# Two small TensorE steps of a Fourier-filter and MLP kernel put into one gap

## The chip, the cores and the metric

The kernel runs on one core of a Trainium2 chip. The metric is the device time of one execution in microseconds, the median of several runs. The core has a matrix engine (TensorE, PE in the profile, with its weight loads as PEld), VectorE (DVE), ScalarE (ACT), GpSimd (POOL) and SyncE (SP), which here only issues DMAs. TensorE writes into eight PSUM banks; VectorE and ScalarE read them out.

## The reference

Eight batches of 3008 tokens with 256 channels each are filtered along the tokens in the frequency domain, and every token then goes through a two-layer MLP with the activation h - tanh(h):

```python
X = np.fft.rfft(x, axis=1)                         # x: (8, 3008, 256)
y = np.fft.irfft(X * (filt_r + 1j * filt_i), n=3008, axis=1)
h = y.reshape(24064, 256) @ w_in                   # (256, 2048)
out = (h - np.tanh(h)) @ w_out                     # (2048, 256)
```

## The kernel before

The transform of length 3008 = 64 x 47 is done as matrix products in three stages. The **first stage** transforms along 64 (`first(b, z)`, six steps for a batch, its products into tiles called `pf`) and stores its result in DRAM (`ct1`). The **middle stage** (`middle(b, z)`) loads it, transforms along 47, multiplies with the filter and transforms back; it has four rounds of ten steps for a batch: "there" (products into four banks), eight filter steps on VectorE, "back" (products into four banks), and its result goes to DRAM again (`ct2`). The **last stage** (`last(i, z)`) loads one group's part of that (`e2`, and a table `gt`), transforms back along 64 (products into `pu`) and so makes the MLP's input `ut` for one group of tokens, with four sums of its blocks (`tu`) on GpSimd.

The MLP is the bulk. Its tokens are cut into 48 groups, six of each batch (c = 0 to 5), of 512 tokens (448 in the first group, c = 0, whose products are 224 wide and not 256). A group is worked off in four units (u = 0 to 3) of a quarter of the hidden width each. Both layers are done by a seven-product scheme for 2 x 2 blocks, so that sums of blocks are needed beside the products: `tu` before the first layer and `t` before the second, both on GpSimd by `combine` (L543 to L546, four subtractions one after another).

Three units are in work at a time. In turn U, `up(U)` makes the first layer's products into the banks x, y and z (L563), `shrink(U - 1)` does the activation (three ScalarE functions L675, L678, L681; a VectorE multiplication L685 for each half; and at its end, behind the second half, the four `t` sums on GpSimd), and `down(U - 2)` makes the second layer's products into the banks o0 to o3 (L733). In the last unit of a group these banks are read out as soon as they are complete, in the turn that is unit 1 of the next group; the last of these sums is L767 on GpSimd, and `store` then transposes the two halves of the output on VectorE (L813) in unit 2 and queues its DMAs.

The order of all engines is written out by hand: each engine works off its instructions in the order in which the program issues them. `up` calls `t(k)` at five places of a unit; these places are the **gaps** (u, k) into which the Fourier steps are put. For a unit of batches 1 to 7 the order is: X1, Y2, `t(0)`, second-layer products, `t(1)`, X6, Z5, second-layer products, `t(2)`, X7, second-layer products, X4, `t(3)`, the last part of the activation, second-layer product 4, `t(4)`, Z3. (X, Y, Z name the bank; Z3 adds onto the bank that L603 reads in between, Z + u3.) At every gap the stores queued by the first stage (`written`) are issued by ScalarE and four of the other queued stores (`outs`) by SyncE.

In batches 1 to 5 a group holds these steps:

- first stage of the batch after next: gap (0, 2), into the banks t and y
- middle stage of the next batch: "there" in (2, 0) of groups 0 to 3, into t, o3, o1, o2; filter steps in gaps of units 2, 3, 0 and 1; "back" in (1, 3) of groups 1 to 4, into o0, t, y, o1. So group 0 has no "back", and group 5 has no step of the middle stage at all
- last stage of the next group: gap (3, 2), into t and y

The first stage's steps do two 64-row halves at once, eight matmuls of 64x64 by 256 columns (L296); one bank is copied by ScalarE (L301), and VectorE takes sum and difference (L302, L303). The last stage's step is 32 matmuls of 64x64 by 64 columns (L522), read out in the same way (L526, L529, L530).

Loads: `load_e2` for the next group is issued at the head of unit 0, but at the head of unit 2 where the next group begins a batch. In unit 2 of group 5 the first loads of the next `middle` and the next `first` are issued too; each further step of `first` issues the loads of the step after next.

Of the kernel before, what the change touches and what calls it, by code (L numbers as in the profile page):

```python
# [9 lines left out]
F32 = mybir.dt.float32  # L10
# [7 lines left out]
BATCH, SEQ, DM = 8, 3008, 256  # L18
# [8 lines left out]
NC = NH // CH  # L27
# [84 lines left out]
def kernel(  # L112
# [32 lines left out]
    groups = [(b, c) for b in range(BATCH) for c in range(NC)]  # L145
# [363 lines left out]
    e2s, uts = {}, {}  # L509
# [425 lines left out]
    with tc.tile_pool(name="tr", bufs=2) as tr, tc.manual_schedule():  # L935
# [257 lines left out]
        with tc.tile_pool(name="dn", bufs=2) as dn, \  # L1193
                tc.tile_pool(name="ps", bufs=1, space=bass.MemoryType.PSUM) as ps:

            def zd(name, shape):
                return ps.tile(shape, F32, tag="t", bufs=1, name=name)

            def zd2(name, shape):
                return [ps.tile(shape, F32, tag=tag, bufs=1, name=name) for tag in "ty"]  # L1200

            def zd4(tags):
                return [ps.tile([128, 2, DM], F32, tag=tag, bufs=1, name="pm") for tag in tags]

            psums.append(zd)
            pairs_of.append(zd2)

            y_sums = dn.tile([128, 2 * 4 * len(groups)], F32, bufs=1, name="y_sums")

            def psl(shape, tag):  # L1210
                return ps.tile(shape, F32, tag=tag, bufs=1, name="pt")

            def filters_d():
                zero = tr.tile([128, 2, DM], F32, tag="e1", bufs=2, name="zero")
                G.memset(zero, 0.0)
                row = 4 * DM
                nc.sync.dma_start(dram(filt_d, 2 * DM, [[PAD * row, 31], [1, 2 * DM]]),
                                  zero[0:31].rearrange("p a n -> p (a n)"))
                for k in range(4):
                    nc.sync.dma_start(dram(filt_d, (NH + 2 * k) * row,  # L1220
                                           [[PAD * row, 32], [2 * DM, 4], [1, 2 * DM]]),
                                      zero.rearrange("p a n -> p (a n)"))
                yield
                for at in range(8):
                    a = 8 * (at // 2) + at % 2
                    n = 4 if at < 7 else 3
                    for v, src in enumerate((filt_r.tensor, filt_i.tensor)):
                        base = at * 128 * row
                        nc.sync.dma_start(dram(filt_d, base + v * DM,
                                               [[row, NH], [PAD * row, n], [1, DM]]),  # L1230
                                          dram(src, (a + 1) * DM,
                                               [[NQ * DM, NH], [2 * DM, n], [1, DM]]))
                        yield
                        nc.sync.dma_start(dram(filt_d, base + row + (2 + v) * DM,
                                               [[row, NH - 1], [PAD * row, n], [1, DM]]),
                                          dram(src, (NQ - a - 1) * DM,
                                               [[NQ * DM, NH - 1], [-2 * DM, n], [1, DM]]))
                        yield
                        if n == 3:
                            nc.sync.dma_start(dram(filt_d, turned * row + v * DM,  # L1240
                                                   [[row, NH], [1, DM]]),
                                              dram(src, 0, [[NQ * DM, NH], [1, DM]]))

            bound = bounded()
            copies = filters_d()
            total = 4 * len(groups)
            for _ in last(0, z2):
                pass
            warm = psl([128, 256], "o3")
            for _ in range(4):  # L1250
                nc.tensor.matmul(warm[0:KM], mats[:, 3 * KM:4 * KM], mats[:, 3 * KM:3 * KM + 256],
                                 start=True, stop=True)
            G.dma_start(mats[:, 0:10 * PAD], wide_d[0:KM])
            for _ in range(4):
                next(late)
            due = [4 + (LEAD - 4) * k / (NX + 4) for k in range(NX + 4)]
            plan = []
            kinds = {(2, 0): "there", (1, 3): "back"}
            kinds.update({at: "filter" for at in FILTERED})

            firsts, mids = {2: fs}, {}
            for U in range(total + 2):
                i, u = divmod(U, 4)
                if U == 6:
                    assert not pending
                    late = sums(7)
                if U < total:
                    p, c = groups[i]
                    if c == 0 and u == 0 and 0 < p < BATCH - 1:
                        plan += STAGES  # L1270
                    if u == 0 and i + 1 < len(groups) and c + 1 < NC:
                        e2s[i + 1] = load_e2(*groups[i + 1])
                    if u == 2 and i + 1 < len(groups) and c + 1 == NC:
                        assert not plan
                        e2s[i + 1] = load_e2(*groups[i + 1])
                    if u == 2 and c + 1 == NC:
                        for gens, ahead, what in ((mids, 2, middle), (firsts, 3, first)):
                            if p + ahead < BATCH:
                                gens[p + ahead] = what(p + ahead, zd4 if what is middle else z2)
                                next(gens[p + ahead])  # L1280
                sh = shrink(U - 1) if 0 <= U - 1 < total else iter(())
                dw = iter(())
                if 0 <= U - 2 < total:
                    dw = (down if U - 2 >= 4 else down_plain)(U - 2)

                def converting(n):

                    for _ in range(n):
                        if next(late, pending) is pending:
                            pending.clear()  # L1290

                def d():

                    next(dw, None)

                def e():

                    next(dw, None)
                    converting(3 if U > 1 else 1)

                def s():

                    next(sh, None)

                def t(k):

                    while written:
                        ACT.dma_start(*written.pop(0))
                    store_some(4)
                    if k == 2 and stores:  # L1310
                        store(*stores.pop())
                    if U >= total:
                        return
                    pos = 20 * c + 5 * u + k
                    if i == 1 and pos == LEAD - 7:
                        mids[1] = middle(1, zd4)
                        next(mids[1])
                        plan.extend(STAGES)
                    if (u, k) == (3, 2) and i + 1 < len(groups):
                        next(last(i + 1, z2))  # L1320
                    elif due and due[0] <= pos and (U < 4 or u < 3 and k == 2):
                        due.pop(0)
                        next(firsts[2])
                    elif (u, k) == (0, 2) and 0 < p < BATCH - 2:
                        next(firsts[p + 2])
                    elif plan and plan[0] == kinds.get((u, k)):
                        plan.pop(0)
                        next(mids[p + 1])
                    converting(2)
                    if k and U > 1:  # L1330
                        next(copies, None)

                if U < total:
                    if U == total - 1:
                        ones = cst.tile([128, 1], F32, name="ones")
                        G.memset(ones, 1.0)
                    (up if U >= 4 else up_plain)(U, d, e, s, t)
                else:
                    for k in range(5):
                        s()  # L1340
                        s()
                        d()
                        if U == total + 1 and k in (0, 2):
                            next(bound)
                        e()
                        t(k)
            for w in stores:
                store(*w)
            store_some(len(outs))
# [36 lines left out]
```

## Time and profile before

| what | value |
|---|---|
| time, median of 3 runs | 2607.54 us (2607.4 to 2609.2) |
| profiled execution, its own time | 2605.47 us |
| span of the profiled execution | 2603.7 us |
| mean granted TensorE clock | 0.995 |
| busy: TensorE / VectorE / ScalarE / GpSimd | 2568.3 / 1911.0 / 1668.0 / 1378.7 us |

A line of a timeline gives the start in us from the begin of the span, the duration in us, the engine, the source line, the operation with the tiles that it writes and reads, and in brackets how long the engine was idle before and what ended that. In the chain (the work that ended last, in order of time) a line is start, duration, engine, tile, source line and the number of records. A line of waits is: engine, its tile and line, `<-`, what it waited for; then us in total, times, and the longest. A float32 matmul leaves two records, so "x4" of L563 is one product of two matmuls. A matmul's record ends after its successor has begun; the chain counts from start to start.

### The profile page before, as it was taken

The numbers are of one execution on the slowest core, as the hardware profiler recorded it, in microseconds if no ns is written. First come the engines' busy times: TensorE is split into PE (matmuls) and PEld (weight loads), VectorE is DVE, ScalarE is ACT, GpSimd is POOL, SyncE is SP. The second block draws the span as 40 slices with busy tenths as digits, with TensorE's granted clock in tenths as the row PEclk, the third lists the DMA queues.
The fourth block names the chain that finished last, engine by engine and source line by source line (L and its number), as shares of the span: only waits on it lengthen the run. The fifth ranks groups of instructions, "written<-read, shape, count | busy, mean of one in ns | idle before, by whom it ended". The sixth has DMA issues, their size and how long they took to land.

```text
span 2603.7 us, 47351 instructions
## 1 busy us (share of the span) xinstructions
PE 2568.3 (99%) x18276; PEld 2201.7 (85%) x18276; DVE 1911.0 (73%) x2514; ACT 1668.0 (64%) x2594; POOL 1378.7 (53%) x1087
## 2 busy tenths in 40 slices
PE   8998999999999999999999999999999999999998
PEld 7677888888898888988889888888889888898887
DVE  6787886888668885788758887588866888555555
ACT  4565666666666666666666666666666666666665
POOL 4114664565546554555555555455654665555552
PEclk9999999999999999999999999999999999999999
DMA  8853315332323323333233432333221331110110
GB/s 224 258 165 99 87 25 124 94 104 61 92 64 106 95 60 82 91 86 98 49 88 84 110 76 55 94 95 93 74 71 41 78 81 36 39 34 18 24 22 18
DMA packets 347852, 214.49 MB, mean 82 GB/s; under 512 B 242179, under 2 KB 315791, under 8 KB 347553
## 3 DMA queue, kind: packets, MB, share of 16 engines
q1 hardware_dynamic: 331601, 174.98, 27.0%
q10 hardware_dynamic: 11632, 23.11, 2.8%
q0 software_dynamic: 4384, 13.29, 1.7%
q8 instruction: 146, 2.39, 0.4%
q14 instruction: 89, 0.73, 0.1%
HBM read 130.72 MB, written 83.39 MB: 82 GB/s over the span
## 4 chain that ended last, share of the span: by engine, by line
PE 94%; DMA 2%; DVE 2%; ACT 1%; POOL 1%; issue 0%; SPq 0%; ACTq 0%; DVEq 0%; POOLq 0%
PE o L733 42%; PE x L563 25%; PE z L563 12%; PE y L563 6%; PE pm L340 3%; PE pu L522 2%; PE pf L296 1%; PE o L788 1%; DMA filt<-in_filt_r_dram 1%; DMA ct<-a 0%; DMA x<-in_x_dram 0%; PE pf L284 0%; DMA ct<-nn 0%; PE o L633 0%; DMA ct<-e 0%
## 5 line engine op out<-in xcount | busy, mean ns | idle before, releaser
L733 PE MATMUL o<-t,wd 128*128 128x256 f32 (+1 forms) x3008 | 762.4, 376 | 0.1
L543 POOL TENSOR_TENSOR t<-h 128x512 f32<-128x512 f32 (+1 forms) x186 | 292.7, 1574 | 761.3 <-DVE h L685 757.4
L685 DVE TENSOR_TENSOR h<-h,y 128x1024 f32<-128x1024 f32 (+1 forms) x384 | 530.8, 1382 | 141.4 <-ACT y L681 140.9
L733 PEld LDWEIGHTS o<-t,wd 128*128 128x128 f32 x3008 | 569.1, 190 | 75.2 <-issue 9.9
L563 PE MATMUL x<-tu,wu 128*128 128x256 f32 (+1 forms) x2256 | 579.0, 379 | 0.0
L733 PE MATMUL o<-h,wd 128*128 128x256 f32 (+1 forms) x2256 | 572.8, 376 | 1.8 <-DVE h L685 1.8
L569 ACT COPY s<-x 128x512 f32<-128x512 f32 (+1 forms) x188 | 108.6, 578 | 602.1 <-PE x L563 571.6
L733 PEld LDWEIGHTS o<-h,wd 128*128 128x128 f32 x2256 | 426.0, 190 | 62.4 <-issue 11.5
L563 PEld LDWEIGHTS x<-tu,wu 128*128 128x128 f32 x2256 | 421.0, 190 | 65.1 <-issue 12.0
L678 ACT ACTIVATE y<-y 128x1024 f32<-128x1024 f32 (+1 forms) x384 | 399.3, 1040 | 12.1
L675 ACT ACTIVATE y<-h 128x1024 f32<-128x1024 f32 (+1 forms) x384 | 400.9, 1044 | 3.6 <-DVE h L611 1.7
L681 ACT ACTIVATE y<-y 128x1024 f32<-128x1024 f32 (+1 forms) x384 | 399.7, 1041 | 5.0 <-ACT a L286 0.4
L544 POOL TENSOR_TENSOR t<-h,t 128x512 f32<-128x512 f32 (+1 forms) x186 | 275.3, 1480 | 14.6
L545 POOL TENSOR_TENSOR t<-h 128x512 f32<-128x512 f32 (+1 forms) x186 | 279.9, 1505 | 0.0
L546 POOL TENSOR_TENSOR t<-h,t 128x512 f32<-128x512 f32 (+1 forms) x186 | 260.6, 1401 | 0.0
L569 ACT COPY u<-x 128x512 f32<-128x512 f32 (+1 forms) x376 | 213.4, 568 | 56.4 <-PE x L563 53.6
L611 DVE COPY h<-x 128x512 f32<-128x512 f32 (+1 forms) x188 | 127.8, 680 | 123.4 <-PE x L563 122.3
L563 PE MATMUL z<-ut,wu 128*128 128x256 f32 (+1 forms) x752 | 191.1, 377 | 9.1 <-DVE h L603 9.1
L563 PE MATMUL x<-ut,wu 128*128 128x256 f32 (+1 forms) x752 | 190.8, 376 | 0.0
L563 PE MATMUL y<-ut,wu 128*128 128x256 f32 (+1 forms) x752 | 190.1, 375 | 0.0
L563 PE MATMUL z<-tu,wu 128*128 128x256 f32 (+1 forms) x752 | 190.0, 375 | 0.0
L586 DVE TENSOR_TENSOR h<-y,s 128x512 f32<-128x512 f32 (+1 forms) x188 | 126.6, 673 | 65.2 <-PE y L563 57.6
(175 smaller groups left out, 2933.4 us busy)
## 6 DMA issues: line engine op xcount, KB each, us to landing
ft<-filt SPq DMA_DIRECT2D x56, 512.0 KB
ct<-nn SPq DMA_DIRECT2D x112, 256.0 KB
e<-ct SPq DMA_DIRECT2D x47, 512.0 KB
a<-ct SPq DMA_DIRECT2D x224, 96.0 KB
out_dram<-ot SPq DMA_DIRECT2D x1248, 16.0 KB
x_sb<-in_x_dram SPq DMA_DIRECT2D x74, 256.0 KB
ct<-a ACTq DMA_DIRECT2D x62, 256.0 KB
gt<-g_pairs SPq DMA_DIRECT2D x42, 128.0 KB
```

The source lines that it names most:

```text
L543: by.tensor_sub(t[0], b[0][1], b[0][0])
L544: by.tensor_sub(t[1], b[1][1], t[0])
L545: by.tensor_sub(t[2], b[1][1], b[0][1])
L546: by.tensor_sub(t[3], b[1][0], t[1])
L563: nc.tensor.matmul(bank[:, k], wu[:, q - 1, (2 * u + k) * 128:(2 * u + k + 1) * 128], rhs[q - 1], start=(first and k == 0), stop=True, ski ...
L569: ACT.copy(t, X)
L611: V.tensor_copy(h[:, 2, :, 0:w], X)
L675: ACT.activation(y[k], ht[k], AF.Arctan, scale=TURN)
L678: ACT.activation(y[k], y[k], AF.Tanh, scale=BEND)
L681: ACT.activation(y[k], y[k], AF.Square, scale=SCALE, accum_out=y_sums[:, 2 * U + k // 2:2 * U + k // 2 + 1])
L685: V.tensor_mul(ht[k], ht[k], y[k])
L733: nc.tensor.matmul(product(q), wd[:, q - 1, (2 * u + k) * 128: (2 * u + k + 1) * 128], rhs[q - 1][:, k], start=(u == 0 and k == 0 and q == ...
```

## The change

In groups 0 and 5 of batches 1 to 5 (ten groups), both the first-stage step, which was in gap (0, 2), and the last-stage step, which was in gap (3, 2), are issued in gap (1, 3), one behind the other. The first-stage step keeps the banks t and y, the last-stage step takes o0 and o1. In groups 1 to 4, and in batches 0, 6 and 7, the two steps stay where they were. With it `load_e2` is issued at the head of unit 0 for the first group of a batch too (but for batch 1's, which stays at unit 2), since the step that reads it comes earlier.

```diff
+            pair = ["ty"]
+
             def zd2(name, shape):
-                return [ps.tile(shape, F32, tag=tag, bufs=1, name=name) for tag in "ty"]
+                return [ps.tile(shape, F32, tag=tag, bufs=1, name=name) for tag in pair[0]]
...
-                    if u == 0 and i + 1 < len(groups) and c + 1 < NC:
-                        e2s[i + 1] = load_e2(*groups[i + 1])
-                    if u == 2 and i + 1 < len(groups) and c + 1 == NC:
-                        assert not plan
+                    if u == (p == 0 and c + 1 == NC) * 2 and i + 1 < len(groups):
+                        assert not plan or c + 1 < NC
                         e2s[i + 1] = load_e2(*groups[i + 1])
...
-                    if (u, k) == (3, 2) and i + 1 < len(groups):
+                    joined = 0 < p < BATCH - 2 and c % (NC - 1) == 0
+                    if joined and (u, k) == (1, 3):
+                        next(firsts[p + 2])
+                        pair[0] = "o0", "o1"
+                        next(last(i + 1, z2))
+                        pair[0] = "ty"
+                    elif (u, k) == (3, 2) and i + 1 < len(groups) and not joined:
                         next(last(i + 1, z2))
                     elif due and due[0] <= pos and (U < 4 or u < 3 and k == 2):
                         due.pop(0)
                         next(firsts[2])
-                    elif (u, k) == (0, 2) and 0 < p < BATCH - 2:
+                    elif (u, k) == (0, 2) and 0 < p < BATCH - 2 and not joined:
                         next(firsts[p + 2])
```

## The prediction

> **What bounds the kernel now.** I read the page's busy shares first, then its chain, then who TensorE waits for (in the stretch from 420 us to 2590 us, where the five changed batches lie), and at last the timeline of the two places that change.
>
> ```profile
> PE 2568.3 (99%) x18276; PEld 2201.7 (85%) x18276; DVE 1911.0 (73%) x2514; ACT 1668.0 (64%) x2594; POOL 1378.7 (53%) x1087
> PE 94%; DMA 2%; DVE 2%; ACT 1%; POOL 1%; issue 0%; SPq 0%; ACTq 0%; DVEq 0%; POOLq 0%
> PE o L733 <- DVE h L685: 1.8, 2, 1.6
> ```
>
> TensorE is busy all the time and the chain is TensorE. The third line is that whole list of TensorE's waits: 1.8 us in two waits. So the change can win only what it takes out of TensorE's own stream, and it loses whatever makes TensorE wait where it does not wait now.
>
> **What a gap costs TensorE.** The chain in order of time, around one last-stage step (`pu`, L522) and one first-stage step (`pf`, L296), each standing alone:
>
> ```profile
> 727.48 1.09 PE pu L522 x64
> 728.57 1.06 PE x L563 x4
> ...
> 731.36 0.86 PE x L563 x4
> ...
> 740.43 1.02 PE pf L296 x16
> 741.46 0.95 PE x L563 x4
> 742.41 1.73 PE o L733 x8
> 744.14 0.76 PE x L563 x4
> ```
>
> The product behind each step is longer than the same product elsewhere: 1.06 for 0.86, 0.95 for 0.76. So `pu` costs 1.09 + 0.20 = 1.29 and `pf` 1.02 + 0.19 = 1.21, together 2.50 us. The change touches ten such pairs.
>
> Back to back, the step into normal products after `pf` goes away: 1.02 + 1.09 + 0.20 = 2.31, 0.19 saved. Perhaps some of the way in goes too. Nothing in this trace has the two steps side by side. Each step by itself reads 1.02 and 1.09; in each quarter of the array both push as many columns as a 256-wide product pair, which takes 0.86, so the joined step lies between 1.72 + 0.20 = 1.92 and the full 2.50. I take 2.24, nearer to the rows as they stand: 0.26 saved for each of ten, 2.6 us in all.
>
> The Trainium skill (TensorEngine Tiling (Array Packing), section Key Properties) says that a change of tiling mode drains the array, and a change of tile alone does not. Both steps are on 64x64 tiles, so by it the junction is free; that is the rival "only the drain", below.
>
> **What follows behind the gap.** The new place is behind the product X4 of unit 1, ahead of the last product of the finished group. First the pace of the evictions, from the two steps as they are now, and the `tu` sums that GpSimd makes of the last stage's result:
>
> ```profile
> 740.36 1.09 PE L296 MATMUL pf<-x_sb,f 64*64 64x256 f32 x16
> 741.52 0.58 ACT L301 COPY other<-pf 128x512 f32<-128x512 f32 x1 [0.56 <-PE pf L296]
> 742.14 0.69 DVE L302 TENSOR_TENSOR a<-pf,other 128x512 f32<-128x512 f32 x1 [1.61 <-ACT other L301]
> 742.75 0.68 DVE L303 TENSOR_TENSOR a<-pf,other 128x512 f32<-128x512 f32 x1
> ...
> 727.41 1.16 PE L522 MATMUL pu<-gt,e 64*64 64x64 f32 x64
> 729.26 0.69 DVE L529 TENSOR_TENSOR ut<-pu,odd 128x512 f32<-128x512 f32 x1 [2.24 <-ACT odd L526]
> 729.87 0.55 DVE L530 TENSOR_TENSOR ut<-pu,odd 128x384 f32<-128x384 f32 x1
> 730.49 0.67 POOL L543 TENSOR_TENSOR tu<-ut 128x224 f32<-128x224 f32 x1 [4.56 <-DVE ut L530]
> 732.47 0.66 POOL L546 TENSOR_TENSOR tu<-ut,tu 128x224 f32<-128x224 f32 x1
> ```
>
> VectorE starts on `pf` 1.78 us after its first matmul and takes 0.61 a step. The second step's copy is ready 1.85 after `pu` starts, which is about 1.0 + 1.85 = 2.85 after `pf` starts, before VectorE has done L302 and L303 (1.78 + 1.22 = 3.0). So four evictions run without a break and L685, the multiplication of unit 1, starts 1.78 + 2.42 = 4.20 after the gap. In both cases `tu` comes about then, and on GpSimd the four `tu` sums now stand **ahead of** the four `t` sums of L685's result, and these ahead of the output sum L767. In the old place, unit 3, the `t` sums were followed by no L767.
>
> Now the first group of a batch (batch 1), as it is:
>
> ```profile
> 443.06 0.92 PE L563 MATMUL x<-tu,wu 128*128 128x224 f32 x4
> 444.59 1.08 DVE L685 TENSOR_TENSOR h<-h,y 128x896 f32<-128x896 f32 x1
> 445.82 1.14 POOL L543 TENSOR_TENSOR t<-h 128x448 f32<-128x448 f32 x1 [1.32 <-DVE h L685]
> 450.32 0.73 POOL L767 TENSOR_TENSOR o<-p,p 128x256 f32<-128x256 f32 x1
> 452.67 1.09 DVE L685 TENSOR_TENSOR h<-h,y 128x896 f32<-128x896 f32 x1
> 453.68 1.30 DVE L813 STREAM_TRANSPOSE ot<-o 128x512 f32<-128x512 f32 x2
> 454.90 1.18 DVE L432 TENSOR_TENSOR nn<-xy,ft 128x1024 f32<-128x1024 f32 x1
> 456.00 0.61 DVE L603 TENSOR_TENSOR h<-z,u 128x448 f32<-128x448 f32 x1
> 457.00 0.92 PE L563 MATMUL z<-ut,wu 128*128 128x224 f32 x4
> ```
>
> The last line, product Z3 of unit 2, writes the bank that L603 reads: it cannot start before L603's end, and the slack today is 457.00 - 456.61 = 0.39 us. L603 stands on VectorE behind the filter step L432, that behind the two transposes L813, and the second transpose needs L767. Today L767 ends at 451.05, and the second transpose comes up at 453.68 + 0.65 = 454.33, 3.3 us later.
>
> How VectorE and GpSimd meet:
>
> ```profile
> 712.59 1.27 POOL L546 TENSOR_TENSOR t<-h,t 128x512 f32<-128x512 f32 x1
> 713.23 1.71 DVE L685 TENSOR_TENSOR h<-h,y 128x1024 f32<-128x1024 f32 x1 [2.19 <-ACT y L681]
> 713.82 1.72 POOL L767 TENSOR_TENSOR o<-p,p 128x256 f32<-128x256 f32 x1
> ...
> 719.49 1.22 DVE L685 TENSOR_TENSOR h<-h,y 128x1024 f32<-128x1024 f32 x1
> ```
>
> L685 takes 1.22 alone and 1.71 here: it ends 1.08 after L546's end (713.86). L767, 0.73 elsewhere, ends at 715.54, so it ran from 714.81: it stood about 0.95 behind L685. One waits for the other in full. The Trainium skill (SBUF — State Buffer, section Who interferes with whom) says the same: a VectorE instruction with two SBUF inputs and a GpSimd one that reads SBUF lock each other out, the earlier one first. Without such holds the two sums below would end 1.8 and 1.9 us earlier, no wait would be left in them, and the change would win 0.26 at each place.
>
> The sum for the first group: `pf` starts behind X4, 443.06 + 0.76 + about 0.1 = 443.9. L685 at 448.1. It holds GpSimd until 449.05 (0.95). Four `tu`: 730.49 to 733.13 is 2.64 for 224 columns; the next group has 256, so 3.0: 452.05. Four `t`: 445.82 to 450.32, 4.5: 456.55. The L685 of unit 2 falls among them and holds them once more, 0.85 for its 896 columns: 457.4. L767 0.73: 458.1. Second transpose 0.65: 458.8. L432 1.10: 459.9. L603 0.61: 460.5. Z3 then starts at 460.5 for 457.00, so 3.5 later; the two steps that are gone from units 0 and 3 give back 2.50. **Net 1.0 us lost.** TensorE by itself would be there at 457.0 + 2.24 = 459.2; it waits 1.3, part of it perhaps earlier, at the middle-stage step at the head of unit 2 (L340), whose bank o3 is read by an add queued behind L685.
>
> The last group (batch 1), which has no filter step in unit 2:
>
> ```profile
> 705.74 1.03 PE L563 MATMUL x<-tu,wu 128*128 128x256 f32 x4
> 708.77 1.27 POOL L543 TENSOR_TENSOR t<-h 128x512 f32<-128x512 f32 x1 [1.60 <-DVE h L685]
> 714.87 1.41 DVE L813 STREAM_TRANSPOSE ot<-o 128x512 f32<-128x512 f32 x2
> 716.91 0.69 DVE L603 TENSOR_TENSOR h<-z,u 128x512 f32<-128x512 f32 x1 [0.64 <-ACT u L569]
> 719.55 1.03 PE L563 MATMUL z<-ut,wu 128*128 128x256 f32 x4
> ```
>
> `pf` at 705.74 + 0.96 = 706.7; L685 at 710.75 (the fourth eviction is the narrow one); GpSimd free at 711.7; `tu` 2.64: 714.35; four `t` 5.05 (708.77 to 713.82): 719.4; one hold 0.95: 720.35; L767 0.73: 721.1; second transpose 0.70: 721.8; L603 0.69: 722.5. Z3 moves by 2.95, less 2.50: **0.45 us lost.** Part of this wait may be met earlier, at the products that read the `t` sums.
>
> Five of each: 5 x 1.45 = 7.3 us. The other batches' rows lie one batch (312 us) on and I take them to be alike.
>
> **Costs taken at nothing.** ScalarE's two evictions: behind them it has nothing to do before the first copy of unit 2, two products later; without that cover their 1.2 us would delay that copy. Its two stores of `a1` wait for L303, and only that copy is queued behind them. The load of the last-stage input `e2` now leaves at the head of unit 0 in both groups. SyncE:
>
> ```profile
> 696.95 3.23 SPq L323 DMA_DIRECT2D a<-ct  x8
> 705.95 0.63 SPq L255 DMA_DIRECT2D x_sb<-in_x_dram  x1
> 715.59 14.51 SPq L840 DMA_DIRECT2D out_dram<-ot  x28
> ```
>
> The loads L323 read what the first stage stores, whose last part now leaves after 706.7 + 3.0 = 709.7, and before in unit 0. So SyncE stands still from 697 to about 712, its 9.6 us of loads end near 722 and the 28 stores run to 737. The loads are read from the middle of the next group on, the stores by nobody. Queued behind them is the `e2` of the next first group, read about 20 us later; that cover gone, the gap there would wait for it, a microsecond for each that it comes late.
>
> **Rivals.** *Only the drain*: GpSimd's lateness is covered, and the kernel is 2.6 us faster: 2604.9. For it: TensorE never waits now, and GpSimd is busy 53%. Against it is the chain above. In the first group it decides if L767 ends by 451.05 + 3.3 + 0.4 + 2.24 = 457.0 (its slack, that of Z3, and TensorE's own shift) and not at 458.1. Chance 0.12. *Half*: the holds overlap or the sums run faster, the first groups lose 0.6 and the last ones win 0.26: 5 x 0.34 = 1.7, 2609.2. Chance 0.2. *More*: VectorE's lateness runs on into the filter steps of unit 3, and the first group loses 2 us instead of 1: 5 x 2.45 = 12.3, 2619.8. For it: these steps fill VectorE there; against: unit 3 is rid of `pu`'s evictions. Chance 0.08. The forecast has 0.6.
>
> **The numbers.** The profiled execution took 2605.5 (span 2603.7); 7.3 on it is 2612.8. The median of the runs is 2607.5, 2.1 above, so the forecast is 2614.8. The range leaves out most of *only the drain* and of *more*: 2607 to 2619. About 0.2%, 5.2 us, is what a measurement can tell from no change: *only the drain* (2.6) and *half* lie within it, with a small part of the forecast; faster by more would need over 0.52 saved a pair, more than a pair has: 0.03. Same 0.35, slower 0.62.
>
> **What would show it.** TensorE waits for L603 before a `z` product ten times, 0.5 to 1.3 us each; `tu` rows on GpSimd straight before `t` rows, the first of them beside L685; L767 some 3 us later against its unit; `pf` and `pu` in one stretch of about 2.1 us. Wrong if TensorE still waits 1.8 us in all, or if the waits are for a DMA.

## The result, and the profile after

The changed kernel takes 2615.6 us (median of 11 runs, 2611.9 to 2618.2) against 2607.6 (11 runs, 2604.8 to 2610.4): 1.0029 times the time of before, 95% interval 1.0022 to 1.0037. The change makes the kernel 8 us slower. The profiled execution has a span of 2612.5 us.

The busy shares and the chain of the page, and TensorE's waits from 420 to 2590 us:

```profile
PE 2570.4 (98%) x18276; PEld 2203.1 (84%) x18276; DVE 1911.4 (73%) x2514; ACT 1668.8 (64%) x2594; POOL 1386.8 (53%) x1087
PE 89%; POOL 4%; DVE 3%; DMA 2%; issue 1%; ACT 1%; SPq 0%; ACTq 0%; DVEq 0%; POOLq 0%
PE z L563 <- DVE h L603: 4.1, 5, 0.8
PE o L733 <- POOL t L545: 1.9, 6, 0.3
PE o L733 <- DVE h L685: 0.2, 1, 0.2
```

TensorE has as much to do as before. GpSimd, which had 1% of the chain, now has 4% of it, VectorE 3% where it had 2%. The waits have the two names that the sum led to: L603, and a `t` sum. Among the waits of TensorE's weight loads, two are new; before, neither is in the list:

```profile
PEld z L563 <- DVE h L603: 7.6, 10, 1.2
PEld pm L340 <- DVE o L766: 1.1, 5, 0.2
```

The first group of batch 1, the timeline around the joined gap:

```profile
442.26 0.92 PE L563 MATMUL x<-tu,wu 128*128 128x224 f32 x4
443.11 1.09 PE L296 MATMUL pf<-x_sb,f 64*64 64x256 f32 x16
444.02 1.11 PE L522 MATMUL pu<-gt,e 64*64 64x64 f32 x64
446.03 0.92 PE L563 MATMUL z<-ut,wu 128*128 128x224 f32 x4
447.29 1.08 DVE L685 TENSOR_TENSOR h<-h,y 128x896 f32<-128x896 f32 x1
447.45 1.51 POOL L543 TENSOR_TENSOR tu<-ut 128x256 f32<-128x256 f32 x1 [3.76 <-DVE ut L530]
448.39 1.79 PE L340 MATMUL pm<-a,mats_sb 24*32 24x256 f32 x64
451.10 1.14 POOL L543 TENSOR_TENSOR t<-h 128x448 f32<-128x448 f32 x1
454.32 1.20 DVE L685 TENSOR_TENSOR h<-h,y 128x896 f32<-128x896 f32 x1
454.52 2.00 POOL L546 TENSOR_TENSOR t<-h,t 128x448 f32<-128x448 f32 x1
456.47 0.73 POOL L767 TENSOR_TENSOR o<-p,p 128x256 f32<-128x256 f32 x1
457.24 0.71 DVE L813 STREAM_TRANSPOSE ot<-o 128x512 f32<-128x512 f32 x1 [1.10 <-POOL o L767]
457.87 1.18 DVE L432 TENSOR_TENSOR nn<-xy,ft 128x1024 f32<-128x1024 f32 x1
458.98 0.61 DVE L603 TENSOR_TENSOR h<-z,u 128x448 f32<-128x448 f32 x1
459.64 1.02 PE L563 MATMUL z<-ut,wu 128*128 128x224 f32 x4 [0.83 <-DVE h L603]
```

To be read from top to bottom as one chain: L685 and the first `tu` sum meet (1.51 for a sum that takes 0.72), the four `tu` sums take until 451.10, the `t` sums follow, the last of them stands behind the next L685 (2.00 for 1.14), L767 comes at 456.47, the second transpose waits 1.10 for it, and Z3 waits for L603. The L340 step at 448.39 takes 1.79. Before, it took 1.49:

```profile
447.04 1.49 PE L340 MATMUL pm<-a,mats_sb 24*32 24x256 f32 x64
```

It has begun, but its products for bank o3 wait: the sum L766, which reads that bank, ends at 448.71, and within the step no weights are loaded from 448.44 to 448.76. In the list of the products this wait does not appear, so that list (6.2 us) is shorter than what is lost.

The last group of batch 1:

```profile
705.97 1.03 PE L563 MATMUL x<-tu,wu 128*128 128x256 f32 x4
718.11 1.26 POOL L545 TENSOR_TENSOR t<-h 128x512 f32<-128x512 f32 x1
719.42 1.56 PE L733 MATMUL o<-t,wd 128*128 128x256 f32 x6 [0.34 <-POOL t L545]
721.31 0.71 DVE L813 STREAM_TRANSPOSE ot<-o 128x512 f32<-128x512 f32 x1 [3.68 <-POOL o L767]
721.95 0.65 DVE L603 TENSOR_TENSOR h<-z,u 128x512 f32<-128x512 f32 x1
722.65 1.13 PE L563 MATMUL z<-ut,wu 128*128 128x256 f32 x4
```

Here the same lateness is met twice: first at the product that reads the third `t` sum, then at Z3, which begins where L603 ends. The eight matmuls from 718.48 on, in which the first wait lies, take 2.34 us where they took 1.72 before; Z3 and the product behind it come another 0.22 late.

For the size, one stretch that holds one last and one first group: from the last "back" step (L340) of a batch to the first one of the next batch. Before, then after, from the timeline of TensorE:

```profile
654.21 1.50 PE L340 MATMUL pm<-xy,mats_sb 24*32 24x256 f32 x64
804.26 1.50 PE L340 MATMUL pm<-xy,mats_sb 24*32 24x256 f32 x64
```
```profile
655.67 1.49 PE L340 MATMUL pm<-xy,mats_sb 24*32 24x256 f32 x64
807.22 1.49 PE L340 MATMUL pm<-xy,mats_sb 24*32 24x256 f32 x64
```

The stretch is 150.05 us before and 151.55 after: 1.50 is lost per batch, 7.5 in five. The stretches of the later batches in each trace agree with this one to 0.03 us, while whole executions of one kernel differ by some 6. So this stretch is the measure for the experiments.

### The profile page after: what moved, and what is told of

Read it like the earlier page. It is cut to its first block, busy times and chain, and to the rows that moved or that the text cites. A ratio compares the mean times of both kernels' runs of the same rounds, so it can differ in the third digit from the quotient of the medians.

```text
span 2612.5 us, 47353 instructions
## 1 busy us (share of the span) xinstructions
PE 2570.4 (98%) x18276; PEld 2203.1 (84%) x18276; DVE 1911.4 (73%) x2514; ACT 1668.8 (64%) x2594; POOL 1386.8 (53%) x1087
## 4 chain that ended last, share of the span: by engine, by line
PE 89%; POOL 4%; DVE 3%; DMA 2%; issue 1%; ACT 1%; SPq 0%; ACTq 0%; DVEq 0%; POOLq 0%
PE o L733 40%; PE x L563 23%; PE z L563 11%; PE y L563 6%; PE pm L340 3%; PE pu L522 2%; PE pf L296 1%; PE o L788 1%; POOL t L544 1%; POOL tu L543 1%; POOL t L543 1%; PE pf L284 1%; POOL t L545 0%; DMA x<-in_x_dram 0%; POOL t L546 0%
## 5 line engine op out<-in xcount | busy, mean ns | idle before, releaser
L685 DVE TENSOR_TENSOR h<-h,y 128x1024 f32<-128x1024 f32 (+1 forms) x384 | 532.0, 1385 | 141.9 <-ACT y L681 141.7
L544 POOL TENSOR_TENSOR t<-h,t 128x512 f32<-128x512 f32 (+1 forms) x186 | 280.3, 1507 | 14.6
L546 POOL TENSOR_TENSOR t<-h,t 128x512 f32<-128x512 f32 (+1 forms) x186 | 270.0, 1451 | 0.0
L603 DVE TENSOR_TENSOR h<-z,u 128x512 f32<-128x512 f32 (+1 forms) x188 | 126.8, 674 | 66.8 <-ACT u L569 64.4
```

Of the source, the lines that this page charges most:

```text
L544: by.tensor_sub(t[1], b[1][1], t[0])
L546: by.tensor_sub(t[3], b[1][0], t[1])
L685: V.tensor_mul(ht[k], ht[k], y[k])
```

## The experiments

**The `tu` sums put back.** The theory is the queue on GpSimd; the rival is that four evictions in one gap make VectorE late by themselves. The gap stays as changed, but the four `tu` sums are issued where they were, in (3, 2) (all line numbers behind are two higher):

```diff
+        uts[i] = (b, tu, w)
+        if late_sums:
+            yield
         combine(b, [tu[:, k, 0:w] for k in range(4)], V if pending else G)
-        uts[i] = (b, tu, w)
         yield
...
-                        next(last(i + 1, z2))
+                        summing = last(i + 1, z2, late_sums=True)
+                        halves[0] = summing
+                        next(summing)
                         pair[0] = "ty"
+                    elif (u, k) == (3, 2) and joined:
+                        next(halves[0])
```

> Both steps in gap (1, 3) as in the change, but the four tu sums are issued in gap (3, 2), where they stood before. Theory (the tu sums queue ahead of the t sums on GpSimd, and so L767, the transposes, L603 and Z3 come late): the waits for L603 and for the t sums go; left are the saving at the junction, about 0.35 us at each place, and in the first group the wait of the middle-stage step for bank o3, about 0.25 us. The stretch from one batch's last back step to the next batch's first one, 150.05 us before and 151.55 changed, becomes about 149.6; the time about 2605.5 (2 us below the kernel before). Rival (four evictions in one gap make VectorE itself late): most of the loss stays, the stretch is above 150.8, the time above 2611.

```profile
654.92 1.49 PE L340 MATMUL pm<-xy,mats_sb 24*32 24x256 f32 x64
804.67 1.50 PE L340 MATMUL pm<-xy,mats_sb 24*32 24x256 f32 x64
448.64 1.79 PE L340 MATMUL pm<-a,mats_sb 24*32 24x256 f32 x64
PE o L735 <- DVE h L687: 1.8, 2, 1.6
```

The stretch is 149.75, the time 2605.3 us (ratio to the kernel before 0.9992, interval 0.9983 to 1.0001: by the time alone it can't be told from the kernel before). The products' waits for L603 and the `t` sums are gone; only the old 1.8 us is listed. In the stretch, the whole loss of 1.50 has turned into a gain of 0.30, with the same four evictions. What is left is the middle-stage step with 1.79: bank o3, as expected. The stretch is still 0.15 longer than expected; the cause of that stays open. The rival falls. The banks o0 and o1 and the earlier `load_e2` are in this run as in the change, so they don't make the loss either.

**One gap later.** Both steps in (1, 4), behind product 4; by then L685, the `t` sums and L767 have been issued. The stores of the first stage are issued at once, since the loads that read them are issued at the head of unit 2:

```diff
-                    if joined and (u, k) == (1, 3):
+                    if joined and (u, k) == (1, 4):
...
+                        while written:
+                            ACT.dma_start(*written.pop(0))
```

> Both steps back to back one gap later, in (1, 4), behind second-layer product 4, with the same four banks; the stores of the first stage's result are issued right behind them. Theory: L685, the t sums, L766 and L767 are now issued ahead of the evictions and of the tu sums, so nothing of the chain is late and o3 is free in time; 0.35 us saved at each of ten places, stretch about 149.35, time about 2604.1. Rival (four evictions in one gap make VectorE late): VectorE has the same four in one gap, Z-bank add and next copies are late, the stretch stays above 150.5.

```profile
655.08 1.49 PE L340 MATMUL pm<-xy,mats_sb 24*32 24x256 f32 x64
804.42 1.49 PE L340 MATMUL pm<-xy,mats_sb 24*32 24x256 f32 x64
445.83 1.14 POOL L543 TENSOR_TENSOR t<-h 128x448 f32<-128x448 f32 x1 [1.33 <-DVE h L685]
449.21 1.49 PE L340 MATMUL pm<-a,mats_sb 24*32 24x256 f32 x64
450.35 0.72 POOL L767 TENSOR_TENSOR o<-p,p 128x256 f32<-128x256 f32 x1
451.04 0.72 POOL L543 TENSOR_TENSOR tu<-ut 128x256 f32<-128x256 f32 x1
```

The stretch is 149.34, 0.71 below that of before, and the time 2603.5 us (ratio 0.9985, interval 0.9976 to 0.9994): faster than both kernels. On GpSimd the order is now `t`, L767, `tu`, and the L340 step is back at 1.49. So the junction by itself saves 0.35 us at each place, and the changed kernel waits 151.55 - 149.34 = 2.21 us in each stretch.

**Each step alone in the gap.** First only the last-stage step in (1, 3), with the first-stage step left in (0, 2); then the other way round:

```diff
-                        next(firsts[p + 2])
...
-                    elif (u, k) == (0, 2) and 0 < p < BATCH - 2 and not joined:
+                    elif (u, k) == (0, 2) and 0 < p < BATCH - 2:
```

> In the ten groups only the last-stage step moves to (1, 3) (banks o0 and o1), the first-stage step stays in (0, 2). No junction, so nothing saved; VectorE has two evictions in the gap and not four. Theory: the tu sums still stand ahead of the t sums, and both ends of the race at Z3 shift by about the same (VectorE 1.15 us earlier, TensorE 0.9 us earlier): stretch about 151.4, time about 2614.5, as slow as the whole change. Rival (evictions on VectorE): with two in the gap the loss is gone, stretch about 150.1, time about 2607.6.

```profile
658.46 1.49 PE L340 MATMUL pm<-xy,mats_sb 24*32 24x256 f32 x64
810.31 1.49 PE L340 MATMUL pm<-xy,mats_sb 24*32 24x256 f32 x64
PE z L563 <- DVE h L603: 4.2, 5, 0.8
PE o L733 <- POOL t L545: 0.9, 5, 0.2
```

The stretch is 151.85, the time 2616.8 us (ratio 1.0037, interval 1.0023 to 1.0051). Half the evictions, no junction, and it is as slow as the whole change or more; the same two waits are there. My figure, 151.4, was 0.45 too small. The rows of this trace have the race at Z3 about as I had put it: counted from X4, L603 ends 1.13 us earlier than in the change in the first group and 1.02 in the last, and TensorE by itself is at Z3 0.86 earlier. With that the waits come to 1.14 and 0.67 us, and without a junction nothing is taken off them: they are the whole 1.80.

```diff
-                        pair[0] = "o0", "o1"
-                        next(last(i + 1, z2))
-                        pair[0] = "ty"
-                    elif (u, k) == (3, 2) and i + 1 < len(groups) and not joined:
+                    elif (u, k) == (3, 2) and i + 1 < len(groups):
```

> In the ten groups only the first-stage step moves to (1, 3), the last-stage step stays in (3, 2). Two evictions in the gap, no tu sums there. Theory: L685 and the t sums are late by 2.3 us against 1.2 us of TensorE, which the slack of 3.3 us at the second transpose covers: stretch 150.05 to 150.15, time as before, 2607.6. Rival (evictions on VectorE): about half of the loss, stretch about 150.8, time about 2611.

```profile
655.75 1.50 PE L340 MATMUL pm<-xy,mats_sb 24*32 24x256 f32 x64
805.83 1.50 PE L340 MATMUL pm<-xy,mats_sb 24*32 24x256 f32 x64
```

The stretch is 150.08, the time 2606.5 us (ratio 0.9998, interval 0.9989 to 1.0007): nothing lost. The two together say that the loss comes with the last-stage step, the one that brings the `tu` sums. They don't separate these sums from the step's own two evictions; the first run, which moves the sums alone, does.

**Each of the two groups alone.** `c % (NC - 1) == 0` becomes `c == 0`, then `c == NC - 1`.

> The change in the first groups alone (gap (1, 3)); the last groups as before. Theory, the two places are independent: the stretch from a batch's last back step to the next batch's first one goes from 150.05 to 151.09, which is 0.35 saved and 1.39 waited in the first group. Rival, the first group is only late because the last group before it was: the stretch stays near 150.

```profile
656.47 1.50 PE L340 MATMUL pm<-xy,mats_sb 24*32 24x256 f32 x64
807.55 1.50 PE L340 MATMUL pm<-xy,mats_sb 24*32 24x256 f32 x64
```

> The change in the last groups alone (gap (1, 3)); the first groups as before. Theory: the stretch goes from 150.05 to 150.52, which is 0.35 saved and 0.82 waited for the t sums and L603. Rival, the last group hands its lateness on to the first group of the next batch: 150.9 or more.

```profile
656.39 1.49 PE L340 MATMUL pm<-xy,mats_sb 24*32 24x256 f32 x64
806.92 1.49 PE L340 MATMUL pm<-xy,mats_sb 24*32 24x256 f32 x64
```

The stretches are 151.08 and 150.53, so 1.03 is lost in a first group and 0.48 in a last one, together 1.51 for the 1.50 of the whole change. The two places are independent. The times, 2612.3 and 2610.4 us, fit, but are of one execution each; the stretches of the later batches in these two traces repeat the figures to 0.03 us.

**Further along the same way: all six groups.** In groups 1 to 4 the "back" step of (1, 3) stands right ahead. `joined` becomes `0 < p < BATCH - 2`, with gap (1, 4).

> Both steps back to back in gap (1, 4) in all six groups of batches 1 to 5, thirty places and not ten; in groups 1 to 4 they follow the middle stage's back step of gap (1, 3), whose four banks they share, with product 4 in between. If nothing waits, 0.35 us at each place: a batch (from one first there step to the next, 312.25 us before) becomes 310.15, the time about 2596.5. In groups 1 to 4 the back step's last evictions may hold the first matmul for 0.1 to 0.3 us: then about 311 a batch and 2600. Rival (VectorE as the limit): back, four evictions and the there step's sums in a row make VectorE late in these groups, and Z3 or Z5 waits 0.4 us or more at each: 312 a batch or more, no gain over the ten places (2603.5).

From the first "there" step of a batch to that of the next, with TensorE's weight loads' wait at `pf`:

```profile
764.62 1.49 PE L340 MATMUL pm<-a,mats_sb 24*32 24x256 f32 x64
1076.20 1.49 PE L340 MATMUL pm<-a,mats_sb 24*32 24x256 f32 x64
PEld pf L296 <- PE o L733: 9.5, 20, 0.5
```

It is 311.58 here; the four batches that can be read so lie between 311.3 and 311.6, and ten places give 311.53. The time is 2603.3 us (ratio 0.9985, interval 0.9976 to 0.9994), that of ten places. So the twenty further places bring next to nothing: in each of them the weights of `pf` come about half a microsecond late. My estimate missed: with a wait of 0.1 to 0.3 us a batch was to come to 311 and the time to 2600, but nearly all of the 0.35 us saved is lost again at each of these places. As a last step I gave the first-stage step the banks t and o0 and the last-stage step o1 and y:

```diff
-                        next(firsts[p + 2])
-                        pair[0] = "o0", "o1"
+                        pair[0] = "t", "o0"
+                        next(firsts[p + 2])
+                        pair[0] = "o1", "y"
```

> As the thirty places in gap (1, 4), but the first-stage step takes the banks t and o0 and the last-stage step o1 and y, in all thirty. In groups 1 to 4 the first matmul waited about 0.5 us for the back step's evictions; t and o0 are freed one copy earlier on each engine than y and o1. If that wait is what ate the saving there, 0.3 us comes back at each of twenty places: a batch becomes about 310.3 us (311.5 with ten places, 311.3 to 311.6 with thirty), the time about 2598. If the loss lies in what follows (the there step behind the gap, VectorE), a batch stays at 311.3 and the time at 2603.

```profile
449.09 1.49 PE L340 MATMUL pm<-a,mats_sb 24*32 24x256 f32 x64
760.16 1.49 PE L340 MATMUL pm<-a,mats_sb 24*32 24x256 f32 x64
PEld pf L296 <- PE o L733: 9.5, 20, 0.5
```

A batch is 311.07 (311.0 to 311.1 in four) and the time 2601.2 us (ratio 0.998, interval 0.9971 to 0.9989), the lowest of all here, though the interval overlaps those of the last run and of ten places. But not for the reason given: the wait before `pf` is the same 9.5 us in 20 times. About 0.1 us a place came back elsewhere. The profile names a product as the releaser that was long issued. The traces offer a better candidate: in both runs bank t is the first that `pf` writes, and in all 20 places of both the weights come 0.07 to 0.12 us behind the end of VectorE's third copy of the "back" step (L451), the one that frees bank t. So the exchange of banks left this limit where it was. No run begins with another bank, so it is not shown.

## Why the prediction was right

2614.8 was forecast and 2615.6 measured, and each step has its row.

- *Junction.* From the end of X4 (442.26 + 0.76) to the place where unit 1's Z3 would have begun without product 4 (446.03 - 0.86) it is 2.15 us; I took 2.24, a choice between two bounds. `pu` begins 0.91 after `pf` and not 1.02. The saving is 0.35 and not 0.26 a place. This term was too small by 0.9 us in all.
- *Evictions.* L685 begins 447.29 - 443.11 = 4.18 after `pf`; 4.20 was forecast.
- *GpSimd's queue.* Hold and `tu` sums, from L685's start on: 447.29 to 451.10, 3.81; the sum had 0.95 + 3.0 = 3.95. `t` sums with the second hold: 451.10 to 456.47, 5.37; the sum had 5.35.
- *From L767 to Z3.* 456.47 to 459.64, 3.17; the sum had 3.09. The whole way from X4 to Z3 is 17.38 in the first group (17.44 forecast) and 16.68 in the last (16.76).
- *Waits.* Without any wait the stretch would be 149.34; 2.21 are waited. The forecast's parts are 1.26 in the first group (1.0 + 0.26) and 0.71 in the last, 1.97. The rows have 1.40 in the first (0.30 at L340, 1.10 at Z3) and 0.84 in the last (0.62 at the product behind the `t` sum, 0.22 at Z3). So the waits and the saving were both a little small, and it is luck that their errors cancel: 1.45 forecast, 1.50 measured in a stretch; 1.0 and 0.45 forecast for the two groups, 1.03 and 0.48 measured with each alone.
- *What would show it.* I said ten waits for L603, 0.5 to 1.3 us each. The weight loads of Z3 do wait ten times, but the products only five times, 0.8 us each; in the last groups most of the wait is taken at the `t` sum, which the prediction mentioned only as possible. And "L767 some 3 us later" contradicts the prediction's own sum, which has it at 457.4 and not 450.3, 7 us later. The sum is borne out: from X4 to L767 it is 14.21 us after and 7.26 before.
- *Costs taken at nothing.* ScalarE is done with the two evictions in time: before its first copy of unit 2 (447.75) it is idle for 1.96 us, waiting for a product. In the changed kernel TensorE's products wait for no DMA in the list above, nor in any experiment with the new load order. SyncE's loads begin at 713.94 and its stores at 723.94 (712 and 722 forecast); that they run late has no effect that these runs show.
- *Rivals.* "Only the drain" was priced at 2.6 us and is what comes out (5 x 0.71 = 3.5 us) as soon as the queue on GpSimd is in order; in the change as made the limit for L767 in the first group was missed: by the prediction it had to end 457.0 - 443.06 = 13.9 us after X4 began, and it ends after 457.20 - 442.26 = 14.9. "Half" and "more" did not occur.

## What to carry to other kernels

Moving a step moves everything that it issues on every engine: a gap that suits the saturated engine can put four small sums in front of a chain that another engine needs sooner, and the slack along that chain decides (here 3.3 us at the second transpose and 0.4 us at its end, for sums that come 7 us later). Before a step is put into a gap, write down for each in-order queue what is issued right behind it, and how soon the last reader of that comes. The cure need not be to give up the move: here a shift by one gap turned 1.50 us lost into 0.71 us won a batch, and issuing the off-path sums later turned it into 0.30 won.

## What the runs showed of the hardware

Two steps on 64x64 tiles back to back cost 2.15 us where the two apart cost 2.50: 0.35 us is saved, as if one way into and out of the tiled products were paid and not two. That GpSimd and VectorE hold each other off is seen again at once: the first `tu` sum takes 1.51 beside L685 and the next 0.72 alone. Not expected was that a late second transpose (3.68 us idle on VectorE in the last group) costs TensorE only some tenths at Z3 there. L603 stands behind it and ends 4.77 us later against X4 (16.63 for 11.86). But before, it ended 1.95 us ahead of Z3, and TensorE itself now comes there 2.15 + 0.62 us later: only the rest of about 0.1 is left as a wait.
